# A kernel's whole order of steps and its PSUM pairs replaced by another order: RWKV-7 attention and a SwiGLU layer on one Trainium2 core

## The chip, the core and the metric

The kernel runs on one core of a Trainium2 chip as one launch. The metric is the device time of a run in microseconds (us); lower is better. Engines are named as in the profile: PE is the matrix engine (PEld its weight loads), DVE the vector engine, ACT the scalar engine, POOL the GpSimd engine, SP the engine that here only issues DMAs. A trailing "q" (SPq) is that engine's instruction queue.

## The reference

All data is fp32, but for the three weight arrays of the second part, whose 64-bit floats the kernel turns into fp32 itself.

```python
# r, k, v, w, a, b: (4, 8, 768, 40) = batch, heads, steps, head dimension
for t in range(S):
    y[:, :, t] = einsum('bhd,bhde->bhe', rt, state)
    Sa = einsum('bhde,bhe->bhd', state, at)
    state = state * wt[:, :, None, :] - einsum('bhd,bhe->bhde', Sa, bt) + einsum('bhd,bhe->bhde', vt, kt)
x = y.transpose(0, 2, 1, 3).reshape(3072, 320)
xn = x / sqrt(mean(x * x, -1) + 1e-6) * rms_g
g, val = xn @ w_gate, xn @ w_val            # (320, 1536) each
out = (g * sigmoid(g) * val) @ w_out        # (1536, 320)
```

## The kernel before, in words

The 768 steps of the recurrence are cut into 24 chunks of 32 steps. Each chunk has three stages. `front` loads the chunk's tokens (tiles `wan`, `kbn`, `wn`, `VU`), turns them with PE transposes, and builds by five levels of doubling the decayed keys and the Gram matrices of the chunk (tiles `K`, `A`, `Ab`, `KN`, `T`, `LT`); at its end LT goes through memory (`sB`) into another layout (`M`). `inverse` copies the constant tile `eye` into `Yi` on ACT and solves a 32-step triangular system in many small DVE operations on `Yi` and `tmp`; the result goes back through memory (`sY`) into LT. `main` carries the state over, solves for the chunk's updates on PE, forms the outputs `y` level by level with masks (`msi`, `msk`), takes their root mean square with a `pow` on POOL (tile `ss`), and lays the normed tokens into `xg`.

The second layer, `feed`, takes the tokens of one or two chunks at a time, in 13 groups (one chunk, eleven times two, one chunk). For each of 12 slices of d_ff it multiplies with the gate and value weights into PSUM (`ps<-xg,wf`), applies Silu on ACT (`sg`), multiplies on DVE (`hT`) and accumulates the output product in a PSUM tile of its own (`po<-wf,hT`).

The weights come as 64-bit floats. `narrow` (L964) loads the raw words of one half of a slice, and takes the exponents apart and rebuilds fp32 with five DVE operations and three ACT operations. There are 24 such halves, numbered from 0; the loads of halves 0 to 3 go through SP's queue, those of halves 4 to 23 through POOL's. Later halves reuse a later slice's tile as their raw buffer, so a load may wait until an earlier half has been narrowed. Once the weights are in, POOL issues nothing but the chunks' token loads and one `pow` per chunk.

Constants and the padding of tiles are made at the start by short POOL fills, copies and selects (`blank` L461, `pcopy` L458, `select` L484). Among them are ten 64x16 copies from `msk` into `msi` and four selects that make `eye`. Nothing fixes when they come, other than their users.

None of these stages issues an instruction when it is written down. Each operation becomes a piece in a list (class `Plan`, L205) with its engine and the pieces it needs; in all there are 5,993 pieces: 2,717 on DVE, 1,113 on ACT, 1,091 on PE (groups of 4 to 64 matmuls), 588 on POOL, 484 on SP. `Plan.issue` (L282) then issues them in the order of a constant, `ORDER` (L32): each word counts from the first piece not yet issued.

```python
for word in order.split():
    i = first + int(word)
    gone.add(i)
    while first in gone:
        first += 1
    p = self.pieces[i]
    assert not p.missing
```

The order of the words decides what stands in each engine's queue, and in what order; each engine works its queue off strictly from the front, so that a waiting instruction holds up all behind it. Semaphore waits follow from what each piece reads and writes. A second constant, `PAIRS` (L185), holds one digit, 0 to 2, for each of the 495 uses of PSUM outside `po`: which of three pairs of PSUM banks that use takes. The next use of a pair must wait until the engines have read the last one's contents. There is no other planner at run time: the two constants were found ahead of time and stand in the source as numbers.

Of the kernel before, what the change touches and what calls it, by code (L numbers as in the profile page):

```python
# [32 lines left out]
76 84 83 86 75 71 2 3 4 5 6 7 0 35 47 0 17 54 64 0 0 51 0 35 0 55 0 0 67 68 60 190 191 41 49 374 59 71 375 0  # L33
35 0 0 0 46 359 380 185 73 0 32 170 171 181 75 74 73 0 1 27 3 0 368 2 0 352 373 343 173 2 167 166 342 72 80 73 85 84 96 69
70 78 83 94 74 365 79 40 53 353 62 371 61 366 354 64 51 52 374 54 81 15 93 75 82 76 92 95 91 367 86 89 90 63 183 77 100 344 168 39
165 297 298 88 104 184 102 106 97 87 105 101 198 108 98 107 348 345 103 185 190 113 99 346 16 656 668 175 176 9 5 31 109 112 368 355 369 116 114 117
115 118 120 119 110 111 347 186 187 122 356 299 359 349 203 370 350 191 657 18 665 4 357 188 197 284 19 17 28 375 121 71 196 376 667 666 43 382 285 377
358 123 202 379 201 213 30 0 401 171 652 41 199 359 379 198 360 25 191 123 300 299 210 124 125 126 127 213 128 211 301 129 192 130 209 203 131 193 132 221
208 206 402 392 654 391 382 390 205 133 207 134 181 657 170 5 194 377 223 219 135 222 136 214 217 137 218 138 204 216 230 393 139 380 225 411 140 141 215 410
413 142 143 226 144 145 383 146 147 148 149 150 151 224 412 234 663 384 235 236 152 385 386 237 168 387 153 155 662 154 156 394 388 403 389 407 395 404 238 239  # L40
240 396 180 414 415 405 406 6 43 318 7 13 433 22 408 398 676 157 432 179 418 399 419 241 416 397 409 229 188 158 159 160 161 400 228 417 452 31 453 244
420 441 443 245 246 434 247 248 444 677 227 242 435 436 243 442 249 220 250 251 252 438 253 254 464 463 169 437 285 454 461 0 460 253 254 437 255 453 284 256
438 456 454 285 286 287 257 482 0 250 251 435 643 447 252 436 449 473 283 280 253 254 281 450 282 255 223 493 256 439 257 258 259 260 261 494 651 437 292 455
438 262 22 662 263 264 440 293 441 456 661 660 1 296 475 457 483 459 479 284 303 458 482 299 460 298 484 285 300 485 461 297 648 665 476 304 302 306 305 222
307 309 477 301 495 310 502 505 650 503 478 664 499 311 221 313 312 266 267 265 268 270 314 504 23 315 486 496 497 763 316 480 271 269 272 764 317 822 821 481
487 498 832 819 676 500 318 488 506 319 490 320 766 544 489 663 501 669 491 507 321 767 322 545 833 768 769 770 536 508 535 829 670 677 323 492 675 682 771 820
525 324 671 772 775 510 680 681 773 692 668 774 534 524 509 325 778 679 678 693 690 688 672 686 765 689 691 673 687 683 779 828 533 16 2 831 827 674 294 699
694 697 511 700 512 526 701 824 830 834 649 823 295 698 702 703 685 527 528 705 684 546 695 782 838 658 0 204 370 380 211 378 203 511 333 205 212 215 206 216
389 390 391 228 467 463 462 460 382 213 381 459 465 464 475 476 214 221 398 222 470 385 383 457 458 388 392 395 393 394 466 461 224 384 469 386 223 217 225 471
450 468 474 752 230 451 226 399 400 401 402 403 404 405 406 407 408 409 410 751 499 249 749 762 759 411 472 412 387 413 473 414 517 250 761 513 415 477 518 416  # L50
417 478 760 418 419 479 420 421 480 422 423 481 424 425 426 427 482 614 615 516 617 510 227 229 509 750 428 629 515 514 396 520 429 431 430 630 432 528 521 397
526 527 522 532 530 529 533 534 523 544 524 531 537 536 541 525 542 538 540 535 543 539 436 434 545 549 553 548 0 553 549 434 545 555 432 550 560 546 554 556
565 566 567 551 558 250 557 230 234 235 518 254 255 231 232 251 617 564 568 571 570 765 615 618 619 233 252 236 559 620 253 770 621 453 569 256 574 771 259 630
257 623 258 260 757 499 575 576 577 578 579 580 581 582 583 584 585 586 587 588 589 590 591 592 593 594 595 596 622 625 624 626 627 597 598 454 746 632 634 633
747 269 764 635 631 0 637 481 0 1 0 478 399 669 679 668 515 558 565 555 516 177 670 556 517 518 519 400 401 181 520 671 178 402 672 564 522 523 521 524
563 562 574 557 477 566 182 179 180 403 567 183 561 568 560 559 573 572 569 570 571 575 576 577 578 579 783 184 844 854 842 841 843 784 682 744 684 685 528 525
526 840 678 852 527 786 683 186 580 187 689 479 404 697 488 407 406 489 696 787 188 788 789 688 690 702 190 849 848 857 405 700 785 713 851 853 839 191 189 701
581 695 790 710 858 791 582 192 850 712 691 583 698 795 584 711 794 724 193 733 709 792 699 847 793 585 692 194 708 798 196 707 693 799 703 195 706 694 723 717
714 719 722 718 704 705 725 715 721 730 0 725 585 715 733 5 196 6 719 734 7 730 726 1 727 736 0 733 6 198 799 0 194 0 547 798 46 799 194 805
0 730 796 543 719 47 728 190 192 803 729 722 798 42 731 799 806 43 44 801 805 48 49 802 795 797 804 50 807 0 763 0 763 689 690 691 692 693 694 695  # L60
767 765 764 766 686 696 768 697 1067 769 803 687 698 770 0 943 942 694 800 766 695 799 767 41 1075 696 802 697 805 1064 698 48 47 813 806 803 1065 1063 1073 699
818 700 817 42 43 0 768 767 1030 657 757 0 4 769 770 784 657 762 5 658 774 0 779 658 762 770 780 775 46 782 791 778 659 781 660 763 776 661 53 52
47 49 54 0 43 759 657 772 784 658 769 659 779 783 788 660 782 661 787 790 662 45 785 664 663 781 50 780 789 791 684 794 665 0 687 746 754 749 639 975
752 753 755 45 0 702 41 424 52 967 42 59 0 572 4 5 710 708 15 382 1 709 384 6 10 7 711 11 383 714 0 10 15 780 11 16 0 573 571 572
570 591 796 799 798 592 780 931 913 717 712 719 713 714 721 715 716 723 718 720 0 0 0 766 781 630 767 914 907 904 631 706 709 710 0 767 905 682 768 0
619 709 710 711 712 713 714 715 716 717 718 719 720 721 722 1 364 894 768 3 769 0 0 1 408 405 341 406 0 356 357 405 358 359 235 311 360 0 414 235
3 360 415 361 236 362 237 363 364 238 365 418 366 367 0 367 428 368 419 394 369 1 430 418 370 238 371 0 0 368 427 0 0 414 418 419 417 421 415 416
423 420 426 430 367 368 543 369 427 431 428 544 545 429 724 370 371 0 431 738 306 432 728 371 538 433 732 434 0 371 434 720 372 538 0 731 434 372 373 0
734 550 537 373 2 376 374 375 377 378 0 718 554 541 2 720 3 542 537 565 727 553 4 725 311 6 547 548 715 730 551 543 312 550 726 552 576 555 563 562
716 560 561 558 723 564 559 7 557 570 544 8 379 9 545 575 380 571 574 13 546 595 378 569 556 566 577 567 568 12 578 584 572 585 582 0 581 9 576 10  # L70
582 5 568 0 568 577 572 383 217 6 579 219 384 569 581 422 578 12 423 220 580 424 654 218 652 425 520 426 653 14 509 655 8 656 585 7 586 587 588 590
589 13 9 591 592 427 593 657 594 595 0 654 591 593 655 594 5 653 10 595 596 597 598 599 600 601 602 603 604 605 606 607 608 609 610 388 658 389 611 577
659 12 578 662 673 663 664 675 668 612 669 665 613 666 667 614 670 671 13 18 14 19 615 676 682 15 20 616 617 618 16 619 620 621 674 672 989 622 677 623
678 680 681 624 679 625 626 982 992 991 979 980 505 981 683 627 628 684 514 629 0 0 0 4 613 668 614 669 615 670 671 616 617 702 706 842 703 575 704 618
619 620 717 707 716 621 709 6 12 722 710 622 624 715 711 623 705 721 719 718 7 733 729 727 744 712 720 731 843 625 728 723 725 730 9 732 713 738 726 13
8 743 14 714 742 737 739 626 734 749 724 10 629 627 745 15 735 639 736 746 748 740 755 747 763 754 756 0 0 962 678 688 741 697 629 742 617 833 661 395
398 397 749 746 748 662 396 747 0 0 657 681 943 954 814 815 658 961 724 829 830 951 828 953 659 626 734 962 671 393 817 0 951 626 817 1 943 398 3 820
# [969 lines left out]
```

## Time and profile before

| | |
|---|---|
| median of 3 runs | 1016.63 us (1014.07 to 1021.52) |
| the profiled execution | 1023.57 us |
| its span, first to last instruction | 1021.8 us |
| mean granted PE clock | 0.943 |
| PE, PEld, DVE, ACT, POOL busy | 930.1, 759.6, 771.4, 509.7, 350.0 us |
| instructions | 55,373 |

"Busy" is the time in which an engine worked on at least one instruction. Matmuls overlap, and their ends are modelled, so PE may be busy and still not at its fastest. In answers of the timeline, a row has the start, the duration, the engine, the source line, the operation, output and input tiles, and in square brackets the engine's idle time before it with what ended it. L423 is the helper that issues nearly all DVE operations, L466 the one that issues DMAs, L469 the one for matmuls and L472 the one for transposes, so it is the tiles that tell one operation from another.

### The profile page before, as it was taken

To read this page: it belongs to the slowest core of one execution; us is meant where nothing else is said; L and a number is where in the kernel's file an instruction comes from. 1 tells how busy PE (TensorE), PEld (TensorE's weight loads), DVE (VectorE), ACT (ScalarE), POOL (GpSimd) and SP (SyncE) were. 2 spreads that over 40 slices of the span, in tenths; PEclk is the share of its full clock that TensorE was granted. 3 is DMA by queue.
4 is the path that set the end of the run, shared out by engine and by line. 5 is a ranking of instruction groups with operands and counts; after the bars stand their busy time and mean duration, and the time that the engine had idled before them with its cause. 6 is when DMAs were issued, how large, how long until landed. Compare 5 with 4: busy or idle time off the path is not lost.

```text
span 1021.8 us, 55373 instructions
## 1 busy us (share of the span) xinstructions
PE 930.1 (91%) x24512; PEld 759.6 (74%) x24512; DVE 771.4 (75%) x2718; ACT 509.7 (50%) x1133; POOL 350.0 (34%) x595
## 2 busy tenths in 40 slices
PE   4366688999989999999999999999999999999998
PEld 4255577878767787788788777778787878788877
DVE  8889877787867966877769779679598697685531
ACT  6788467445445544465353454454544545435121
POOL 8988363242324314315133143143133224210000
PEclk9557767999999999999999999999999999999999
DMA  8574453323324324133232142242232323320100
GB/s 172 149 190 115 96 110 74 68 47 60 54 58 78 56 53 75 36 71 61 45 81 44 44 95 39 55 84 49 43 72 51 75 50 66 67 35 7 43 8 20
DMA packets 140175, 68.87 MB, mean 67 GB/s; under 512 B 120768, under 2 KB 127264, under 8 KB 139936
## 3 DMA queue, kind: packets, MB, share of 16 engines
q0 software_dynamic: 19680, 32.48, 15.9%
q1 hardware_dynamic: 118080, 32.54, 15.4%
q8 instruction: 192, 3.15, 1.3%
q10 hardware_dynamic: 2176, 0.33, 0.2%
q14 instruction: 47, 0.39, 0.1%
HBM read 55.05 MB, written 10.22 MB: 64 GB/s over the span
## 4 chain that ended last, share of the span: by engine, by line
PE 55%; DVE 24%; DMA 7%; issue 5%; POOL 4%; ACT 3%; SPq 2%; DVEq 0%; ACTq 0%; POOLq 0%
PE ps L469 40%; PE po L469 10%; PE ps L472 5%; DVE Yi L423 4%; DVE LT L423 3%; DVE y L423 3%; DVE tmp L423 3%; DVE K L423 3%; DMA sB<-LT 3%; SPq L466 2%; DVE As L423 2%; DMA M<-sB 2%; DVE Ab L423 1%; POOL wf L466 1%; DVE hT L423 1%
## 5 line engine op out<-in xcount | busy, mean ns | idle before, releaser
L469 PE MATMUL ps<-xg,wf 128*128 128x256 f32 (+3 forms) x1872 | 364.5, 377 | 1.5 <-ACT sg L446 0.8
L469 PEld LDWEIGHTS ps<-xg,wf 128*128 128x128 f32 (+1 forms) x1872 | 271.1, 191 | 48.6 <-issue 8.1
L469 PE MATMUL po<-wf,hT 128*128 128x320 f32 x576 | 179.0, 444 | 0.2 <-issue 0.2
L469 PEld LDWEIGHTS po<-wf,hT 128*128 128x128 f32 x576 | 103.5, 189 | 35.6 <-issue 1.4
L423 DVE TENSOR_TENSOR tmp<-Yi,M 128x24 f32<-128x24 f32 (+21 forms) x512 | 107.2, 209 | 12.1 <-DMA M<-sB 1.6
L423 DVE TENSOR_TENSOR Yi<-Yi,tmp 128x24 f32<-128x24 f32 (+21 forms) x512 | 106.8, 209 | 10.4
L423 DVE TENSOR_TENSOR hT<-ps,sg 128x256 f32<-128x256 f32 (+1 forms) x156 | 60.6, 399 | 63.7 <-PE ps L469 41.4
L446 ACT ACTIVATE sg<-ps 128x256 f32<-128x256 f32 (+1 forms) x156 | 54.5, 368 | 103.3 <-PE ps L469 102.4
L466 POOL DMA_DIRECT2D kbn<-in_k_dram x92 | 53.6, 585 | 146.9 <-PE ps L469 146.2
L466 POOL DMA_DIRECT2D kbn<-in_b_dram x92 | 53.8, 587 | 131.2 <-PE ps L469 130.1
L423 DVE TENSOR_TENSOR K<-K,T 128x256 f32<-128x256 f32 (+1 forms) x191 | 92.8, 499 | 3.7 <-PE ps L469 2.8
L469 PE MATMUL ps<-Ab,K 64*60 64x56 f32 (+2 forms) x4608 | 79.4, 224 | 17.5 <-ACT r L450 4.8
L469 PEld LDWEIGHTS ps<-Ab,K 64*60 64x60 f32 (+2 forms) x4608 | 72.6, 136 | 29.0 <-issue 9.3
L423 DVE SCALAR_TENSOR_TENSOR Yi<-M,Yi 128x31 f32<-128x31 f32 (+6 forms) x228 | 43.2, 243 | 66.7 <-DMA out_dram<-o 23.3
L450 ACT COPY KN<-ps 128x640 f32<-128x640 f32 x95 | 65.6, 692 | 46.7 <-PE ps L472 12.9
L466 POOL DMA_DIRECT2D VU<-in_v_dram x92 | 54.1, 590 | 88.0 <-PE ps L469 86.3
L423 DVE TENSOR_TENSOR As<-ps,msi 128x256 f32<-128x256 f32 (+1 forms) x168 | 70.7, 455 | 11.9 <-PE ps L469 7.0
L469 PEld LDWEIGHTS ps<-As,KN 128*40 128x40 f32 x3072 | 67.3, 128 | 15.2 <-issue 5.3
L469 PE MATMUL ps<-As,KN 128*40 128x32 f32 x3072 | 72.0, 208 | 6.1 <-DVE As L423 2.9
L466 POOL DMA_DIRECT2D wn<-in_w_dram x92 | 52.4, 571 | 69.6 <-DVE KN L423 65.4
L450 ACT COPY K<-K 128x512 f32<-128x512 f32 x95 | 60.2, 634 | 23.7 <-PE ps L469 10.9
L456 POOL TENSOR_TENSOR ss<-ss,mhalf 128x1 f32<-128x1 f32 x24 | 18.1, 755 | 147.1 <-DVE ss L423 146.9
(137 smaller groups left out, 1526.4 us busy)
## 6 DMA issues: line engine op xcount, KB each, us to landing
M<-sB SPq DMA_DIRECT2D x96, 128.0 KB, 2.9
wan<-in_r_dram SPq DMA_DIRECT2D x24, 160.0 KB, 4.2
kbn<-in_b_dram POOLq DMA_DIRECT2D x92, 40.0 KB, 2.5
VU<-in_v_dram POOLq DMA_DIRECT2D x92, 40.0 KB, 2.7
wan<-in_w_dram POOLq DMA_DIRECT2D x46, 80.0 KB, 3.0
wan<-in_a_dram POOLq DMA_DIRECT2D x46, 80.0 KB, 2.8
kbn<-in_k_dram POOLq DMA_DIRECT2D x92, 40.0 KB, 2.7
wn<-in_w_dram POOLq DMA_DIRECT2D x92, 40.0 KB, 2.9
```

Of the source, the lines that this page charges most:

```text
L423: plan.add("DVE", time + more + each * size(o), 0.087, lambda at: [fn(at(o), *m(at))], [o], aps(*args))
L446: scalar(o, [a], lambda at: nc.scalar.activation(at(o), at(a), f, **kw), aps(acc), 0.1 if f in (AF.Square, AF.Relu) else 0.0)
L450: scalar(o, [a], lambda at: nc.scalar.copy(at(o), at(a)), extra=more)
L456: plan.add("POOL", 0.5, 0.06, lambda at: nc.gpsimd.tensor_tensor(o, a, b, op), [o], [a, b])
L466: plan.add(by, 0.6 if by == "POOL" else 0.45, 0.0, lambda at: queue.dma_start(out=o, in_=i), [o], [i], load=load, since=since)
L469: return o, lhsT, rhs, lambda at: nc.tensor.matmul(at(o), lhsT, rhs, start=start, stop=stop, skip_group_check=True), 4
L472: return o, i, ident, lambda at: nc.tensor.transpose(at(o), i, ident), 2
```

## The change

`ORDER` and `PAIRS` hold other numbers. All 150 lines of the order and all 5 of the pairs change: of the order's 5,993 words 279 are the same at the same position. Nothing else in the file differs; the list of pieces, what each does and what each needs is the same. The order was searched anew as a whole, the early part included, with twelve draws of noise at a time and with a model in which the PE clock follows the work. The diff, cut to the first and last lines of each constant:

```diff
 ORDER = """
-76 84 83 86 75 71 2 3 4 5 6 7 0 35 47 0 17 54 64 0 0 51 0 35 0 55 0 0 67 68 60 190 191 41 49 374 59 71 375 0
...
+388 86 84 2 61 75 3 0 80 81 70 3 4 45 5 6 24 191 200 75 71 84 73 57 7 8 82 26 193 0 78 370 0 5 56 40 0 0 0 375
...
+31 20 0 0 8 0 10 5 18 31 0 13 19 0 13 3 15 9 0 0 0 0 5 0 2 4 0 0 0 2 0 0 0
 PAIRS = """
-212020210212120201011000000002122102121202002110201212101120120100121021022021021012211022112120021122201112110120220200
...
-112220222120210
+100101122202001210212110021002002202122111102010210202010120220121021021020101021021021212221210210012121221002020020200
...
+202001002210021
```

What the new numbers do to each engine's queue is told where the prediction needs it.

More of the change, by code (lines that the diff above doesn't have):

```diff
@@ L32 @@
 ORDER = """
[150 rows of a table removed]
[150 rows of a table added]
 """
 PAIRS = """
-212020210212120201011000000002122102121202002110201212101120120100121021022021021012211022112120021122201112110120220200
-211101012202202011120000200020220222022111222002110010201111111221020101112100110011110120101220200212221202210202000120
-200001010122101111022221020102022012211212111120001012110101122002220000222011120101011110101020010100212121202001201010
-202022202022012001121220211222122020022201202021101121220111201111101001012220112210102111212102000010100200202021210201
-112220222120210
+100101122202001210212110021002002202122111102010210202010120220121021021020101021021021212221210210012121221002020020200
+110121011220020200010212121110110111211000222221002101201022202221012021020202020221012120012121211101102020020122101221
+210110101211202220201120121011020011120020221111010120201212210022020011110000212020022221202120002021222121212112121211
+212121010020120200010100011010100102212121020212101001020100102220110001021220110120202011012120012121210220212022001201
+202001002210021
 """
```

297 rows, old and new, of the table ORDER are left out of this document.

## The prediction

> **What bounds the kernel now.** I read the page first, then the busy time by stretches, then the chain that ended last, then the waits of single instructions in the timeline.
>
> ```profile
> span 1021.8 us, 55373 instructions
> PE 930.1 (91%) x24512; PEld 759.6 (74%) x24512; DVE 771.4 (75%) x2718; ACT 509.7 (50%) x1133; POOL 350.0 (34%) x595
> PE   4366688999989999999999999999999999999998
> PEclk9557767999999999999999999999999999999999
> PE 55%; DVE 24%; DMA 7%; issue 5%; POOL 4%; ACT 3%; SPq 2%; DVEq 0%; ACTq 0%; POOLq 0%
> ```
>
> The kernel has two regimes. The fortieths are 25.5 us each: for the first seven PE is half busy and its granted clock lies between 0.5 and 0.8 (the first slice apart), after that PE is busy throughout at full clock. Shares over the whole span hide this, so here are the stretches (columns: stretch, its length, busy time of each engine, clock, DMA).
>
> ```profile
> 0.00:51.00 51.00, 20.46 (x678) 18.56 (x680) 45.49 (x139) 34.40 (x61) 45.58 (x85) 0.77 0.72 160
> 51.00:102.00 51.00, 32.08 (x1303) 28.73 (x1301) 45.40 (x131) 41.75 (x81) 43.01 (x69) 0.63 0.63 153
> 102.00:153.00 51.00, 37.08 (x1415) 33.42 (x1411) 41.89 (x139) 28.73 (x61) 24.47 (x42) 0.66 0.47 103
> 153.00:204.00 51.00, 47.05 (x1483) 41.41 (x1487) 37.74 (x126) 31.14 (x74) 15.99 (x28) 0.90 0.34 71
> ...
> 408.00:510.00 102.00, 99.18 (x2502) 79.47 (x2501) 79.78 (x311) 47.98 (x110) 28.71 (x49) 1.00 0.27 52
> ...
> 970.00:1022.00 52.00, 47.24 (x646) 38.40 (x644) 12.65 (x36) 11.61 (x33) 0.55 (x1) 0.99 0.06 14
> ```
>
> Up to 102 us DVE (45.5 and 45.4 of 51) and POOL (45.6 and 43.0 of 51) are the full engines. From 204 us on PE is: 99.2 of 102 in the stretch shown. So a reordering can save in two places: DVE's idle time before 204 us, which is 5.51 + 5.60 + 9.11 + 13.26 = 33.5 us by these rows, and the few per cent that PE idles later. The chain shows that the early bound is not DVE alone:
>
> ```profile
> 28.86 0.22 POOL msi L459
> 29.09 3.54 issue
> 32.62 0.73 POOL wf L466
> ...
> 50.55 4.14 DMA wf<-in_moe_w_gate_dram
> ```
>
> From 28.9 to 54.7 us everything that ended last was POOL's queue: fills of tiles, small copies and the issue of weight loads one behind the other, and at its end a load that lands just as DVE needs it. The timeline says why POOL was late (square brackets: idle time before it and what ended it):
>
> ```profile
> 7.30 0.65 POOL L466 DMA_DIRECT2D wan<-in_w_dram  x1 [1.38 <-PE ps L472]
> 9.91 0.33 POOL L459 COPY msi<-msk 64x16 f32<-64x16 f32 x1
> 27.53 0.74 POOL L466 DMA_DIRECT2D wf<-in_moe_w_gate_dram  x1 [2.46 <-DVE A L423]
> 28.51 0.68 DVE L423 TENSOR_TENSOR K<-K,T 128x512 f32<-128x512 f32 x1
> 28.86 3.81 POOL L459 COPY msi<-msk 64x16 f32<-64x16 f32 x1
> 32.62 0.73 POOL L466 DMA_DIRECT2D wf<-in_moe_w_gate_dram  x1
> ```
>
> The same 64x16 copy took 0.33 us at 9.91 and 3.81 us at 28.86, where DVE ran one operation on two tiles behind another. With the two waits for a free buffer, 1.38 and 2.46 us, POOL lost 7.3 us ahead of the load at 50.55.
>
> **The change, part by part.** No instruction is added or taken away: both programs have the same 13,464 matmuls, 2,717 planned DVE steps, 1,113 of ACT, 588 of POOL and 484 of SP. What moves, counted in the two orders with the durations of this execution:
>
> *Balance.* By the first step of feed 0, DVE has done 171.0 us of its work in the old order and 171.8 in the new, and PE 62.6 and 62.6 (at its median late pace). By the last step of feed 1 it is 285.5 and 280.0. PE's sequence has 537 runs of one stage before and 545 now. So the plan is the same and this is a local shuffle: DVE steps move by about 1 us, PE steps by 2 to 6. A gain or loss of tens of microseconds has no source here.
>
> *DVE, early.* I counted the DVE steps that stand less than 2 us of DVE work behind the step of another engine that they need, within the first 172 us of DVE work: 85 before, 58 now. Each is a place where a small lateness stops DVE and all behind it. The largest waits of before show what was done:
>
> ```profile
> 39.39 0.29 DVE L423 TENSOR_TENSOR Ab<-Ab,T 128x128 f32<-128x128 f32 x1 [2.34 <-PE ps L469]
> 69.22 0.76 DVE L423 TENSOR_TENSOR As<-ps,msi 128x256 f32<-128x256 f32 x2 [1.31 <-PE ps L469]
> 88.19 0.74 DVE L423 COPY_PREDICATED LT<-near,ps 128x384 f32<-128x384 uint32 x1 [1.94 <-ACT VU L450]
> 105.39 0.42 DVE L423 TENSOR_TENSOR y<-y,ps 128x256 f32<-128x256 f32 x1 [0.95 <-ACT y L450]
> 134.04 0.19 DVE L423 TENSOR_TENSOR tmp<-Yi,M 128x30 f32<-128x30 f32 x1 [1.58 <-DMA M<-sB]
> 162.68 0.75 DVE L423 COPY_PREDICATED LT<-near,ps 128x384 f32<-128x384 uint32 x1 [1.13 <-PE ps L469]
> 200.38 0.29 DVE L423 TENSOR_TENSOR hT<-ps,sg 128x128 f32<-128x128 f32 x1 [3.04 <-ACT sg L446]
> ```
>
> Ahead of the first four the new order puts 1.26, 2.55, 2.15 and 4.15 us more DVE work, enough for 1.26 + 1.31 + 1.94 + 0.95 = 5.5 us of them; ahead of the last three it puts nothing, or takes work away. Done for all 25 early waits over 0.25 us (25.6 us together), the work put ahead covers 12.9 us. That is the best case, because the work put ahead was taken from another place, where a wait can open. From the other side the number of tight places gives 33.5 x (1 - 58/85) = 10.6 us. The worst case without a new mechanism is 0: waits that only change place. I take half of 10.6, **-5.3 us**, because DVE's total is unchanged and the balance at feed 0 is the same in both orders.
>
> *POOL, early.* Two things go for it. The 3.81 us copy moves from 24.4 to 8.0 us of POOL work, ahead of the dense DVE stretch; at 0.33 us it saves 3.5. The loads that waited 1.38 and 2.46 us now stand 7.1 and 8.6 us of POOL work later, so those waits should end. Against it: loads of weights go back in POOL's queue. The gate load of half 4 (the first whose loads POOL issues) has 31.8 us of POOL work ahead instead of 23.2, half 7's last 44.2 instead of 39.8, half 8's (the one at 50.55) 48.0 instead of 46.3, halves 16 to 18 some 5 us more. At half 8 the sum is +1.7 - 1.38 - 2.46 - 3.5 = -5.6 us at best, +1.7 at worst. Since DVE waits for this load, the gain is part of the 5.3 above and not added to it: **0**.
>
> The Trainium skill has the reason for the 3.81 us in "GPSIMD Engine Reference", section 8 (Key points): GpSimd shares its SBUF interfaces with VectorE and contends with DVE instructions that have two SBUF inputs. The trace agrees (0.33 against 3.81 us). The rule also speaks against the change, as the first rival shows.
>
> *PE, late.* Here cover got thinner. PE steps less than 1 us of DVE work behind what they need, after that same 172 us: 70 before, 81 now; PSUM pairs handed on with no PE work between the last read of the old contents and the first write of the new: 132 of 492 before, 144 now. What such waits cost PE after 204 us (us in total, times, longest):
>
> ```profile
> PE ps L469 <- issue: 6.4, 8, 2.3
> PE ps L469 <- DVE hT L423: 3.1, 3, 2.6
> PE ps L469 <- DVE LT L423: 2.9, 8, 0.5
> PE ps L472 <- DVE hT L423: 1.2, 2, 1.0
> PE ps L469 <- DMA LT<-sY: 1.1, 1, 1.1
> PE ps L469 <- DVE As L423: 0.8, 2, 0.4
> ```
>
> Together 15.5 us. Grown by 11/70 that is +2.4 us; against that ACT's tight places fall from 304 to 289, and the lower bound is a like gain, -1.5. I take half of the upper bound, **+1.2 us**. What is queued behind such a wait is all of PE.
>
> *Clock.* PE was busy 32.1 us at clock 0.63 and 37.1 at 0.66 between 51 and 153 us. If closer packing raised 0.66 to 0.76 there, 37.1 us would shrink by some 4.9. But PE idles in these stretches (18.9 and 13.9 us) and PE's early sequence is nearly the same, so I take 0 and keep 5 on either side inside the cases below.
>
> *Sum.* The profiled execution took 1023.57 us, 6.94 above the median of the three runs, so differences are applied to both: 1023.57 - 5.3 + 1.2 = 1019.5 for that execution, 1016.63 - 4.1 = **1012.5 us** for the median.
>
> **The rivals.**
>
> *POOL starves in another place (slower, 1028 us).* In the new order two of the msi copies and three of the four selects that build `eye` stand between 23.5 and 29.8 us of POOL work. That is where DVE runs its two-tile operations back to back, and ahead of the loads of halves 4 and 6. All five read SBUF. If four of them take 3.5 us more each, and one such stall is gone, POOL is 10.5 us later; the copy of `eye` into Yi, which opens inverse 0, and then every weight load are late by that much, and DVE stops in order behind them.
>
> ```profile
> 30.75 0.41 ACT L450 COPY Yi<-eye 128x256 f32<-128x256 f32 x1
> ```
>
> The groups of both kinds of POOL instruction (count | busy us, mean ns of one | idle before):
>
> ```profile
> L485 POOL TENSOR_SCALAR_AFFINE_SELECT eye<-eye 32x256 f32<-32x256 f32 x4 | 2.4, 612 | 0.2
> L459 POOL COPY msi<-msk 64x16 f32<-64x16 f32 x10 | 6.6, 670 | 0.3
> ```
>
> 1016.63 + 10.5 + 1.2 = 1028.3. Against it: the four selects took 612 ns on average though DVE was busy 45.49 of the first 51 us, and nine of the ten copies took (6.6 - 3.81)/9 = 0.31 us. It decides from the fourth long stall on; with one or two the forecast stands.
>
> *All the cover counts (faster, 1005 us).* If the 12.9 us of covered waits come through whole and PE's late waits grow by 1.2, the time is 1016.63 - 11.7 = 1004.9. For it: the first thing that PE needs to fill up is DVE's early work. Against it: it asks that no new wait opens.
>
> *Nothing comes of it (1017.8 us).* The early waits change place, PE is full from 204 us on whatever came before, and only the +1.2 stays. For it: equal balance at feed 0.
>
> **How the numbers follow.** Forecast of a small gain 0.38, nothing 0.20, both within 1% (10.2 us, about what a measurement of this kernel can tell from no change). Full cover 0.25, which is faster by over 1%. POOL's starving and what else costs over 1%, 0.17. So faster 0.25, same 0.58, slower 0.17. The range begins with full cover and a late gain of 1.5 instead of the loss (1016.63 - 12.9 - 1.5 = 1002.2) and ends at 1025, short of the slow rival's price; about 1 in 10 lies outside on either side.
>
> **What would show it.** Right: DVE's idle time before 204 us falls from 33.5 to about 28; the 3.81 us copy is back near 0.33; the half 8 gate load is issued before 50.55; PE's late waits grow by 1 to 2 us; the first long full-clock stretch begins at nearly the same place, some microseconds earlier. Wrong: a POOL copy or select of over 3 us between 24 and 32 us, DVE waiting for POOL or for DMA of wf in the first 100 us, or PE's idle time after 204 us up by more than 5 us. Then the sum's early or late term has the wrong sign.

## The result, and the profile after

The new order is slower by a little: 1025.18 us against 1016.11 us (medians of 18 runs each), a ratio of 1.0079 with a 95% interval of 1.0052 to 1.0105. That is 8.0 us on the 1016.63 us of before; the two medians lie 9.1 us apart. The forecast was 4.1 us in the other direction. Ratios and shares, here and below, leave out single executions over 1.5% above the fastest of their kernel; medians and ranges of times keep them.

| | before | after |
|---|---|---|
| median of 18 runs (lowest to highest) | 1016.11 us (1012.96 to 1024.36) | 1025.18 us (1019.86 to 1031.31) |
| the profiled execution | 1023.57 us | 1025.81 us |
| its span | 1021.8 us | 1024.0 us |

The profiled execution of before lies 7.5 us above its own median and that of after only 0.6 above, so that the two profiles differ by 2.2 us where the kernels differ by 8.0. A loss of a few microseconds is not to be read from these two spans, only where it is local and large.

The page of after, the same rows as those shown of before (busy time, PE's busy tenths and granted clock in fortieths, shares of the chain that ended last):

```profile
PE 932.1 (91%) x24512; PEld 760.4 (74%) x24512; DVE 770.7 (75%) x2718; ACT 507.5 (50%) x1133; POOL 348.3 (34%) x595
PE   4456688999999999999999999999999999999998
PEclk9556757999999999999999999999999999999999
PE 52%; DVE 23%; DMA 7%; issue 7%; POOL 4%; SPq 3%; ACT 3%; DVEq 0%; POOLq 0%; ACTq 0%
```

Nothing shows on this scale: busy times agree within 2.3 us. The difference begins in the stretches of after (length; busy time of PE, PEld, DVE, ACT, POOL; clock; DMA):

```profile
0.00:51.00 51.00, 21.69 (x681) 19.77 (x683) 42.24 (x133) 31.98 (x57) 46.25 (x86) 0.77 0.68 148
51.00:102.00 51.00, 31.07 (x1226) 27.94 (x1226) 47.28 (x127) 41.58 (x80) 40.15 (x66) 0.63 0.63 157
102.00:153.00 51.00, 36.37 (x1340) 33.08 (x1340) 42.52 (x142) 30.85 (x63) 22.08 (x37) 0.64 0.44 99
153.00:204.00 51.00, 45.67 (x1455) 40.02 (x1451) 39.36 (x127) 29.88 (x68) 20.00 (x34) 0.83 0.34 70
```

In the first 51 us DVE was busy for 42.24 us where it had been 45.49, and it caught up later (47.28 against 45.40). Its idle time before 204 us is 8.76 + 3.72 + 8.48 + 11.64 = 32.6 us; it was 33.5. So nearly all of the 5.3 us that DVE was to gain is absent, and it lost 3.25 us in the first stretch. Nor is this idle time a measure of the loss: by 204 us DVE had even done 0.9 us more work than before (171.4 against 170.5), while the results of feed 0, shown below, came 5.6 us later.

The timeline of after says where. POOL first, with one instruction that took as long as ten of its kind:

```profile
9.15 0.19 POOL L459 COPY msi<-msk 64x16 f32<-64x16 f32 x1
...
28.11 0.65 POOL L466 DMA_DIRECT2D wan<-in_w_dram  x1 [2.19 <-PE ps L472]
28.81 6.42 POOL L485 TENSOR_SCALAR_AFFINE_SELECT eye<-eye 32x256 f32<-32x256 f32 x2
35.27 0.95 POOL L462 MEMSET rE<- 32x1024 f32 x1
```

The copy into `msi` that had taken 3.81 us is indeed at 0.19. But two selects of `eye` took 6.42 us together; taken singly, the first ran 5.94 us and the second 0.44. What stood behind them shows in the queues of ACT and DVE, first after, then before:

```profile
36.25 1.01 ACT L450 COPY rE<-ps 104x1024 f32<-104x1024 f32 x1 [4.12 <-POOL rE L462]
37.16 0.41 ACT L450 COPY Yi<-eye 128x256 f32<-128x256 f32 x1
34.02 0.43 DVE L423 TENSOR_TENSOR K<-K,T 128x256 f32<-128x256 f32 x1
37.60 0.19 DVE L423 TENSOR_TENSOR tmp<-Yi,M 128x30 f32<-128x30 f32 x1 [3.15 <-ACT Yi L450]
```

```profile
35.60 1.01 ACT L450 COPY rE<-ps 104x1024 f32<-104x1024 f32 x1 [3.83 <-POOL rE L462]
32.52 0.21 DVE L423 TENSOR_TENSOR tmp<-Yi,M 128x30 f32<-128x30 f32 x1
```

Before, ACT copied `eye` into `Yi` at 30.75, ahead of the copy into `rE`. In the new order the copy into `rE` stands ahead of it, and that one needs POOL's fill of `rE`, which stands behind the selects. So `Yi` was ready at 37.57 and DVE stood still for 3.15 us with the first operation of inverse 0, which begins at 37.60 instead of 32.52. The chain of after runs through the same four rows (start, length, what; of the first select this view counts 3.07 us, and puts the rest down to issue):

```profile
28.81 3.07 POOL eye L485
...
35.27 0.95 POOL rE L462
36.25 0.05 ACT rE L450
...
37.16 0.41 ACT Yi L450
```

How long this stays can be followed by the stores of the feeds' results, whose issues on SP's queue end each feed (feeds 0, 1 and 2; first after, then before):

```profile
214.73 1.72 SPq L466 DMA_DIRECT2D out_dram<-o  x4
290.33 1.77 SPq L466 DMA_DIRECT2D out_dram<-o  x4
371.49 3.11 SPq L466 DMA_DIRECT2D out_dram<-o  x4
```

```profile
209.18 2.02 SPq L466 DMA_DIRECT2D out_dram<-o  x4
285.44 2.11 SPq L466 DMA_DIRECT2D out_dram<-o  x4
365.67 1.87 SPq L466 DMA_DIRECT2D out_dram<-o  x4
```

The new order is 5.6 us late at feed 0, 4.9 at feed 1 and 5.8 at feed 2. At feed 3 the old order issues its four stores singly, from 435.27 to 444.34, and the new one in two pairs, at 435.51 and 436.97, so that from there on single stores no longer compare the two. Nor does one execution stand for its kernel: another trace with the old order up to 470 us (e10, below) has feed 0 at 205.46 and feed 2 at 356.94. So the parts were run by themselves.

PE's waits after 204 us in after (us in total, times, longest):

```profile
PE ps L469 <- issue: 5.2, 8, 1.2
PE ps L469 <- ACT sg L446: 1.8, 3, 0.9
PE ps L472 <- issue: 1.5, 3, 0.7
PE ps L469 <- DVE As L423: 1.1, 2, 0.6
PE ps L472 <- DVE hT L423: 1.1, 3, 0.7
PE ps L469 <- DVE A L423: 1.0, 2, 0.8
```

They sum to 11.7 us where the six largest of before had 15.5.

### The profile page after: what moved, and what is told of

Read it like the earlier page. It is cut to its first block, busy times and chain, and to the rows that moved or that the text cites. A ratio compares the mean times of both kernels' runs of the same rounds, so it can differ in the third digit from the quotient of the medians.

```text
span 1024.0 us, 55383 instructions
## 1 busy us (share of the span) xinstructions
PE 932.1 (91%) x24512; PEld 760.4 (74%) x24512; DVE 770.7 (75%) x2718; ACT 507.5 (50%) x1133; POOL 348.3 (34%) x595
## 3 DMA queue, kind: packets, MB, share of 16 engines
q8 instruction: 192, 3.15, 1.3%
## 4 chain that ended last, share of the span: by engine, by line
PE 52%; DVE 23%; DMA 7%; issue 7%; POOL 4%; SPq 3%; ACT 3%; DVEq 0%; POOLq 0%; ACTq 0%
PE ps L469 38%; PE po L469 10%; PE ps L472 5%; DVE y L423 4%; DVE Yi L423 4%; SPq L466 3%; DVE As L423 3%; DVE tmp L423 3%; DVE LT L423 2%; DMA sB<-LT 2%; DMA M<-sB 2%; DVE K L423 2%; DMA sY<-Yi 1%; DVE hT L423 1%; POOL kbn L466 1%
## 5 line engine op out<-in xcount | busy, mean ns | idle before, releaser
L469 PE MATMUL ps<-Ab,K 64*60 64x56 f32 (+2 forms) x4608 | 82.1, 227 | 19.9 <-ACT r L450 5.8
L423 DVE SCALAR_TENSOR_TENSOR Yi<-M,Yi 128x31 f32<-128x31 f32 (+5 forms) x228 | 43.1, 242 | 48.5 <-DMA M<-sB 32.6
L469 PEld LDWEIGHTS ps<-As,KN 128*40 128x40 f32 x3072 | 66.8, 128 | 15.5 <-issue 6.3
L456 POOL TENSOR_TENSOR ss<-ss,mhalf 128x1 f32<-128x1 f32 x24 | 15.6, 652 | 165.1 <-DVE ss L423 154.3
```

The costliest lines, as they stand in the source:

```text
L423: plan.add("DVE", time + more + each * size(o), 0.087, lambda at: [fn(at(o), *m(at))], [o], aps(*args))
L456: plan.add("POOL", 0.5, 0.06, lambda at: nc.gpsimd.tensor_tensor(o, a, b, op), [o], [a, b])
L469: return o, lhsT, rhs, lambda at: nc.tensor.matmul(at(o), lhsT, rhs, start=start, stop=stop, skip_group_check=True), 4
```

## The experiments

**Where the loss sits.** The theory: the loss is made before 180 us, by POOL's starved selects and what is queued behind them, and carried to the end. The rival: it is made later, by new waits between PE, ACT and DVE. The two orders hold the same set of pieces in their first 1,123 words (up to some 180 us) and again in their first 2,903 (some 470 us), so their parts can be exchanged at these two seams. The digits of `PAIRS` go with their part (in some of these kernels with the pairs' numbers exchanged, so that a pair fits across the seam). Written with the two orders as lists:

```diff
-ORDER = old[0:1123] + old[1123:2903] + old[2903:]
+ORDER = new[0:1123] + old[1123:2903] + old[2903:]   # e1_first_new
+ORDER = old[0:1123] + new[1123:2903] + new[2903:]   # e2_rest_new
```

> The first 1,123 pieces (to about 180 us, the same set of pieces in both orders) in the new order, the other 4,870 in the old one. Theory (two eye selects on POOL starve at 28.8 us, inverse 0 starts 6.4 us late, and the lag stays to the end): 5 to 6.5 us slower than before, 1021 to 1023. Rival (the loss is made after 180 us by thinner cover of PE and the other PSUM pairs): as before, within 1.5 us.

> The first 1,123 pieces in the old order, the rest with its PSUM pairs in the new one. Theory: what is left of the 9 us, 2.5 to 4 us slower than before, 1018.5 to 1020. Rival (late loss): 8 to 9 us slower, 1024 to 1025. If the late part of the new order is as good as the old one: within 1.5 us of before.

> The kernel before, unchanged, as a control and for a second profile. All theories: ratio 1.00 within 0.3%. In the first profile of it the granted clock fell to half for 3.4 us at 297, 400 and 727 us; if those belong to that one execution, this profile has fewer, and a span near 1014.

e4_old_again is the kernel before without any edit, as a measure of what this comparison can tell. All against 1016.96 us of before on that chip:

| | median | ratio | interval |
|---|---|---|---|
| new up to 1,123, old behind | 1025.33 us | 1.0074 | 1.0040 to 1.0108 |
| old up to 1,123, new behind | 1026.47 us | 1.0080 | 1.0048 to 1.0112 |
| before again | 1017.98 us | 1.0024 | 0.9989 to 1.0059 |

Either part alone costs as much as the whole change. So the early part is guilty, and the rest too, which the theory had put at 2.5 to 4 us, and the two losses do not add up: 0.74% and 0.80% apart, 0.79% together.

The second profile of before, taken from e4_old_again, fell on its slowest execution (1027.17 us). Its span is 1025.4 us and not the 1014 that were expected of it, and the clock falls to 0.50 again near 297 and 731 us, though not near 400.

**The parts by themselves.** To get rid of what the rest does, the program is cut off at the seams; everything behind the cut, and with it most of the output, is left out.

```diff
-        for word in order.split():
+        for word in order.split()[:1123]:    # e5_old_1123, e6_new_1123
+        for word in order.split()[:2903]:    # e7_old_2903, e8_new_2903
```

> Only the first 1,123 pieces of the old order (all else, the whole output included, is left out): how long the early part takes by itself. By its trace the old order is through these at about 180 us; with launch and drain some 185 to 200 us. It is the base for the next kernel.

> The same 1,123 pieces in the new order, all else left out. Theory (the early part loses by POOL's starved selects, in every execution): 5 to 7 us over the old order's. Rival (the early lag is one of the profiled execution; the loss comes later): within 2 us of the old order's.

> Only the first 2,903 pieces of the old order (the same set as in the new one; four groups of the output's thirteen are written, the rest left out). By the profiles some 480 us. It is the base for the next kernel.

> The same 2,903 pieces in the new order. By the two profiles the early lag of 5.5 us is caught up by 440 us: then within 1.5 us of the old order's. If it is not caught up in the executions without that lucky stretch, 5 to 9 us over the old order's; then the middle of the old order is what is faster in the timed runs than in its profile.

| | median (lowest to highest) | share of before, interval |
|---|---|---|
| old, 1,123 words | 182.87 us (181.95 to 185.21) | 0.1793 (0.1785 to 0.1801) |
| new, 1,123 words | 189.26 us (187.10 to 189.48) | 0.1854 (0.1844 to 0.1865) |
| old, 2,903 words | 474.19 us (469.17 to 478.98) | 0.4637 (0.4611 to 0.4663) |
| new, 2,903 words | 478.68 us (474.54 to 482.46) | 0.4698 (0.4671 to 0.4725) |

The early part loses 6.4 us, and of that 4.5 us are left at 470 us. This is no matter of which execution was profiled: the runs of the two short kernels don't overlap. The starved select is in the new one's trace again, as is its price on DVE:

```profile
28.76 6.46 POOL L485 TENSOR_SCALAR_AFFINE_SELECT eye<-eye 32x256 f32<-32x256 f32 x2
37.58 0.19 DVE L423 TENSOR_TENSOR tmp<-Yi,M 128x30 f32<-128x30 f32 x1 [3.15 <-ACT Yi L450]
```

In the old one the copy into `msi` that had taken 3.81 us stands at nearly the same time with the same operations on DVE, and takes 0.72:

```profile
28.82 0.72 POOL L459 COPY msi<-msk 64x16 f32<-64x16 f32 x1
```

So how long such an instruction starves differs between two executions of one order. Over all traces that have the old order of POOL up to there, this copy took 3.80 to 3.89 us in six and 0.71 or 0.72 in four. The select of the new order took 5.94 to 6.09 us in all four traces that have it.

**The middle and the end alone.**

```diff
-ORDER = old[0:1123] + old[1123:2903] + old[2903:]
+ORDER = old[0:1123] + new[1123:2903] + old[2903:]   # e9_mid_new
+ORDER = old[0:1123] + old[1123:2903] + new[2903:]   # e10_end_new
```

> Pieces 1,124 to 2,903 (about 180 to 470 us) in the new order with its PSUM pairs, the rest in the old one. If the new order is worse late in one place, this or the next kernel shows nearly all of the 9 us of the kernel with the whole rest new, 1024 to 1026, and the other is as before within 2 us. If the loss is spread over the late part, each shows about half, 1020 to 1022.

> Pieces from 2,904 on (after 470 us) in the new order with its PSUM pairs, those before in the old one. Loss in one place: 1024 to 1026 here or in the kernel above, and the other one within 2 us of before. Loss spread: 1020 to 1022 in both.

Against 1011.17 us of before on that chip: the middle alone 1018.14 us, ratio 1.0066 (1.0035 to 1.0097); the end alone 1017.19 us, ratio 1.0042 (1.0004 to 1.0080). Each of the three parts costs by itself, 0.74%, 0.66% and 0.42% (the last is little more than the 0.24% that the unchanged kernel showed), and together they cost 0.79%. A lag that is made early is thus not simply carried to the end, and what a part costs depends on what it follows.

**Is it the starved select?** The four selects go straight behind the fill of `eye`, ahead of DVE's dense stretch; all else stays as in the new order. Once whole, once cut at 1,123 words (the rest left out).

```diff
 # POOL's queue, by pieces
 fill eye
+select eye, select eye, select eye, select eye
 ...
-select eye   # one at 16.66 us, one at 24.43, two at 28.81
```

> The new order with one thing moved: the four selects that make eye stand right behind the fill of eye in POOL's queue (at about 16 us), not two of them at 28.8 us. Theory: each takes under 0.8 us there, the copy of eye into Yi comes at about 31 us as before the change, and the kernel is 4 to 6 us faster than the new order, 1019 to 1021. Rival (weight loads stand later in POOL's queue, which alone makes narrowing late): under 1.5 us faster than the new order, 1024 to 1025.

> The first 1,123 pieces of the new order with the four selects of eye right behind its fill; all else, the output included, left out. Theory (the starved selects are the early loss): 3.5 to 5.5 us under the new order's 189.3, so 184 to 186. Rival (the weight loads that stand later in POOL's queue are): 188 to 189.5.

The whole kernel took 1026.72 us, ratio 1.0086 (1.0051 to 1.0121): nothing regained, where 4 to 6 us were expected. Yet in its trace nothing stalls (the last of the `msi` copies before the fill of `rE`, the first inverse operation, and the stores of feeds 0 and 2):

```profile
25.78 0.26 POOL L459 COPY msi<-msk 64x16 f32<-64x16 f32 x1
33.61 0.18 DVE L423 TENSOR_TENSOR tmp<-Yi,M 128x30 f32<-128x30 f32 x1
210.53 2.08 SPq L466 DMA_DIRECT2D out_dram<-o  x4
372.28 3.08 SPq L466 DMA_DIRECT2D out_dram<-o  x4
```

It is 4.2 us ahead of after at feed 0 and 0.8 us behind it at feed 2, in an execution of 1027.07 us. The early stall was avoided here, and by these two executions what came of it was gone again before 375 us. That agrees with e2, where the old first part in front of the new rest did not help either.

The cut one took 184.32 us (182.61 to 189.35), share 0.1823 (0.1813 to 0.1834): by the shares, 0.0031 of the 0.0061 that the new order had lost, half; by the times 4.9 of 6.4 us, on another chip. Its profiled execution stands apart: it took 189.35 us, as long as the new order, and the five others 182.61 to 184.97. Its trace shows how the whole loss can come back (POOL, then DVE):

```profile
16.18 2.03 POOL L485 TENSOR_SCALAR_AFFINE_SELECT eye<-eye 32x256 f32<-32x256 f32 x4
26.20 7.79 POOL L459 COPY msi<-msk 64x16 f32<-64x16 f32 x1
35.30 0.95 POOL L462 MEMSET rE<- 32x1024 f32 x1
33.52 0.41 DVE L423 TENSOR_TENSOR K<-K,T 128x256 f32<-128x256 f32 x1
37.63 0.19 DVE L423 TENSOR_TENSOR tmp<-Yi,M 128x30 f32<-128x30 f32 x1 [3.70 <-ACT Yi L450]
```

The selects now take 2.03 us, all four. The next instruction that reads SBUF, the copy that took 0.26 us in the whole kernel, starved in their place, and the fill of `rE` was as late as ever. The last DVE operation of the dense stretch ends at 33.93, and the starved copy at 33.99; in after these are 34.45 and 34.75, in before 32.60 and 32.67. In these executions the starved instruction came through when DVE's stretch of long operations was over, so its price was what was left of that stretch. In the new order the stretch ends only when DVE has run out of work that does not need POOL. What is missing of the loss in the five other executions this trace cannot tell.

**Is starving enough?** The other way round: the old order, cut at 1,123 words (the rest left out), with the copy into `msi` moved to 10 us and two selects of `eye` put in its place at 28.9 us. The copy into `Yi` stays ahead of the one into `rE`.

```diff
 # POOL's queue of the old order, by pieces
+copy msi     # near 10 us
 ...
-select eye, select eye
 ...
-copy msi     # 28.86 us
+select eye, select eye
```

> The first 1,123 pieces of the old order with three POOL pieces exchanged: two selects of eye stand where the msi copy of 3.8 us stood (28.9 us), and that copy goes ahead to 10 us; all else left out. Theory: the two selects take 5 to 7 us there, Yi<-eye comes at 34 to 36 us, and it ends 2 to 5 us over the old order's 182.9, at 185 to 188. Rival (place of the selects does not matter, POOL has slack): 182 to 184.

It took 183.11 us (180.61 to 184.25), share 0.1796 (0.1783 to 0.1809): no loss against 0.1793, where 2 to 5 us were expected. In the one traced execution, of 183.50 us, the selects starve:

```profile
28.38 4.51 POOL L485 TENSOR_SCALAR_AFFINE_SELECT eye<-eye 32x256 f32<-32x256 f32 x2
32.93 0.41 ACT L450 COPY Yi<-eye 128x256 f32<-128x256 f32 x1 [2.38 <-POOL eye L485]
33.37 0.19 DVE L423 TENSOR_TENSOR tmp<-Yi,M 128x30 f32<-128x30 f32 x1 [1.26 <-ACT Yi L450]
```

`Yi` comes 0.4 us behind the selects, and DVE waits 1.26 us instead of 3.15. Two late selects alone cost little: the traced execution of e5, where nothing starved for long, took 183.53 us. Three of the other executions here took 180.61 to 182.72 us, and whether their selects starved is not known, so that a price of up to some 2 us is not ruled out. The larger price must come from what is queued between them and `Yi`: in the new order the fill of `rE` and the copy into `rE`, and a longer dense stretch (5.94 us left of it instead of 4.03).

**All of it taken out.** The new first part with all selects and the three late `msi` copies straight behind the fill of `eye`, and the fill of `rE` straight behind that of `r`; once with the old rest, once cut at 1,123 words (the rest left out).

```diff
 # POOL's queue of the new order, by pieces
 fill eye
+select eye x4, copy msi x3
 ...
 fill r
+fill rE
 ...
-copy msi x3, select eye x4, fill rE   # from their later places
```

> The first 1,123 pieces in the new order with POOL's readers out of the dense stretch (the four selects of eye and the three msi copies still open stand behind the fill of eye at 16 us, the fill of rE behind that of r at 24 us), the rest in the old order. Refined theory (any POOL piece that reads SBUF between 26 and 33 us starves, and in the new order the fill of rE, the rE copy and then Yi<-eye on ACT are queued behind it): the early lag is gone, 1016 to 1019, within 3 us of before. Rival (the rest of the new early order is slower as well, or a new first part costs the old rest its pace): 1022 to 1025.

> The same first 1,123 pieces alone, all else left out. Refined theory: within 1.5 us of the old order's 182.9, and no POOL piece over 2 us before 35 us. Rival (POOL's later weight loads): 185 or more.

The cut kernel took 184.78 us (183.48 to 185.86), share 0.1826 (0.1814 to 0.1838), 1.9 us over e5 where at most 1.5 were expected. The starving is gone from its trace, and `Yi` is ready at 31.98:

```profile
16.18 2.20 POOL L485 TENSOR_SCALAR_AFFINE_SELECT eye<-eye 32x256 f32<-32x256 f32 x4
30.66 1.01 ACT L450 COPY rE<-ps 104x1024 f32<-104x1024 f32 x1
31.57 0.41 ACT L450 COPY Yi<-eye 128x256 f32<-128x256 f32 x1
```

By the shares it has back (0.1854 - 0.1826)/(0.1854 - 0.1793) = 46% of the early loss, by the absolute times 70%; the chips differ. The traced execution has all of it back: 183.48 us, where the traced one of e5 took 183.53 and that of e6 189.48. Of e14's other three, one took 183.71 us and two took 185.85 and 185.86. With the old rest it took 1015.23 us, before 1012.02, ratio 1.0035 (1.0003 to 1.0067), where the unmended first part had 1.0074 (1.0040 to 1.0108). That too is half, but the two intervals overlap. What the slower two executions of e14 lose has no cause found.

**Does the old order gain from the same medicine?** Old order, the 3.81 us copy moved to 10 us, nothing else.

```diff
 # POOL's queue of the old order, by pieces
+copy msi     # near 10 us
 ...
-copy msi     # 28.86 us
```

> The old order with one piece moved: the msi copy that took 3.8 us at 28.9 us goes ahead to 10 us in POOL's queue. Theory (the starved POOL piece costs the old order too): 1 to 3.5 us faster than before. Rival (the weight load behind it waited for nothing that is late, or the next reader starves in its place): within 1 us of before.

1012.10 us against 1012.02, ratio 0.9988 (0.9959 to 1.0018): nothing, where 1 to 3.5 us were expected. In the old order the stall costs nothing that the time shows.

**The middle: order or PSUM pairs?** Old first part and new middle, cut at 2,903 words (the end left out); then the same with 55 of the middle's 153 PSUM uses given to the pair that has been free for longest; and the old order with the same cut on the same chip.

```diff
-ORDER = old[0:1123] + old[1123:2903]                            # e18_old_2903_again
+ORDER = old[0:1123] + new[1123:2903]                            # e15_oldnew_2903
+ORDER = old[0:1123] + new[1123:2903], 55 uses on another pair   # e17_oldnew_other_pairs_2903
```

> The first 1,123 pieces in the old order, 1,124 to 2,903 in the new one, all else left out. Theory (the new order has its own slower pace between 180 and 470 us, which an early lag hides behind): 3.5 to 6.5 us over the old order's 474.2, as late as the wholly new one. Rival (times add up, so the new middle gains what the new start loses): 0 to 3 us under the old order's.

> The first 1,123 pieces in the old order, 1,124 to 2,903 in the new one, as in e15, but each PSUM use of the middle takes the free pair that was left longest ago: 55 of the middle's 153 uses follow another one than the new pairs say. All else left out. If the new pairs make the middle slow: 2 to 5 us under e15 (ratio 0.4703), so 0.465 to 0.468. If the order does: as e15, 0.469 to 0.472, or slower.

> The first 2,903 pieces of the old order once more, all else left out, on the same chip as the kernel above. All theories: the ratio of e7, 0.464 within 0.003; its distance to e17 is what order and pairs of the new middle cost.

The new middle with its own pairs took 475.98 us, share 0.4703 (0.4676 to 0.4730); with other pairs 476.08 us, share 0.4657 (0.4633 to 0.4682); the old order 475.40 us, share 0.4656 (0.4631 to 0.4681). The last two, on one chip, are the same. The one with its own pairs ran on a chip where the kernel before was faster (1012.02 against 1018.61 us), and its absolute time is that of the second. By the shares the pairs would be the cause, by the times they make no difference. The traces side with the times: e15 and e17 (476.79 and 477.95 us) store feed 2 at 370.22 and 371.32, and e18 at 363.15, though it is hardly faster in the end. This stays open.

## Why the prediction was wrong, point by point

**Early DVE, -5.3 us: wrong sign.** This is the step that failed. Counting places where DVE stands close behind its supplier said that 85 places had become 58. But a place is not a price: one place that got worse, `Yi` behind `rE` behind the selects, cost a wait of 3.15 us and put inverse 0 back by 5.1 us, and the early part lost 6.4 us in all. Nor was the gain hidden under the stall: with the stall taken out, the new early order is level with the old one in the traced executions (183.48 against 183.53 us) and 1.9 us behind it by the medians (e14 against e5). DVE's idle time before 204 us, forecast at 28, is 32.6. DVE's largest waits before 204 us in after are (us in total, times, longest):

```profile
DVE LT L423 <- PE ps L469: 5.0, 7, 1.6
DVE tmp L423 <- DMA M<-sB: 3.7, 2, 2.3
DVE tmp L423 <- ACT Yi L450: 3.2, 1, 3.2
```

The first two had been 4.0 and 1.6 us in the same view of before, and the third was not there; the wait of 2.34 us ahead of `Ab` is gone. That is the prediction's worst case, waits that only change place, and a new mechanism on top.

**Early POOL, 0: wrong.** Moving POOL's pieces alone gave back 4.5 of the 6.4 us by the medians and 6.0 us in the traced executions (e14 against e6, on different chips). The two things that spoke for POOL came true: the copy fell to 0.19 us, and the two loads that had waited for a free buffer started without a wait, at 10.10 and 36.75. But another `wan` load now waits 2.19 us, at 28.11. The gate load of half 8, to start before 50.55 if the gain came, is issued at 53.15, past the bound of +1.7 us, and DVE waits a little more for it than the 0.25 us of before:

```profile
53.15 0.78 POOL L466 DMA_DIRECT2D wf<-in_moe_w_gate_dram  x1
57.76 0.41 DVE L423 TENSOR_SCALAR o<-wf 128x480 int32<-128x480 int32 x1 [0.71 <-DMA wf<-in_moe_w_gate_dram]
```

But by then `Yi` had already cost its 3.15 us. What mattered first was which instruction of another engine stands behind which POOL piece, and the sum had looked only at weight loads.

**The rival "POOL starves in another place": right in its place and mechanism, wrong in price and in the point from which it decides.** It named the selects of `eye`, the stretch and the copy into `Yi`. It took 3.5 us for each of four instructions and let the rival decide from the fourth long stall on. In after a single instruction stalled, for 5.94 us, and that sufficed. The stalls do not add up one by one: the first to stall takes what is left of DVE's dense stretch, and those behind it run when the stretch is over (0.44 us for the second select). And the price at the end was not the stall but the queue behind it: with a stall and `Yi` next in line it cost nothing to some 2 us (e12); with a longer stall, and `rE` in between as well, it cost about half of 6.4 us or more (e14 against e6). The rival's 1028.3 us is 3.6 us above what 1.0079 makes of 1016.63 us; part of the closeness is chance, since its term of 10.5 us stood for 6.4 early.

The Trainium skill, "GPSIMD Engine Reference", section 8 (Key points), says that GpSimd contends with VectorE for its SBUF interfaces where DVE reads two inputs. The traces agree: what starved were the reading instructions (5.94 us for a select of 0.44, 7.79 us for a copy that took 0.26 in e3), while in after the fill of `LT` at 25.39 took 0.52 us and the issue of the load at 28.11 took 0.65 us. In the same stretches stood single DVE operations that read one tile (0.41 us, as at 29.86 and 32.09 in after), and the select did not come through there.

**Late PE, +1.2 us: too small.** The new middle alone cost 0.66% and the new end alone 0.42%, some 6.7 and 4.3 us of 1016.63. Behind the new first part they cost together some 0.5 us (0.79% less 0.74%) to 1.6 us (the 8.0 of the whole less the 6.4 of the first part by itself), both within the noise. The sign that was to show it, PE's waits grown by 1 to 2 us, pointed the wrong way: 15.5 us fell to 11.7 in the six largest rows. The base itself was not sound: late waits differ between executions of one order by more than the forecast. One wait of DVE in before, and the same in e10, which has the same order up to 470 us:

```profile
289.44 2.48 DVE L423 SCALAR_TENSOR_TENSOR Yi<-M,Yi 128x27 f32<-128x27 f32 x12 [8.07 <-DMA out_dram<-o]
```

```profile
281.94 2.48 DVE L423 SCALAR_TENSOR_TENSOR Yi<-M,Yi 128x27 f32<-128x27 f32 x12 [4.73 <-DMA M<-sB]
```

DVE waited 8.07 us in one and 4.73 in the other for LT's way through memory into `M` (the first row names the store queued right behind M's loads, which took 4.3 to 4.7 us to land). The multiplication into `hT` stands behind it, and PE behind that: the 2.6 us in the row of before's waits. In the six traces with this order up to there (in e16 but for one POOL copy), the wait is 6.85 to 8.19 us in four and 4.71 and 4.73 in two. The six largest rows of PE's waits sum to 15.5 us in before and to 16.7 in the second trace of the same kernel (e4), but to 11.3 in e16. So the fall to 11.7 shows no gain, and scaling the six rows by a count of tight places asked more of one execution than it can tell.

**Clock, 0:** the first stretches have 0.77, 0.63 and 0.64 against 0.77, 0.63 and 0.66, as taken. From 153 to 204 us it is 0.83 against 0.90, with PE busy for 45.67 us instead of 47.05: there the lag shows, PE fills up later.

**What stays open:** what is left of the early loss by the medians (in e14 and e13), the mechanism of the middle's and the end's losses, and why three losses of 0.74, 0.66 and 0.42% make 0.79% together. The stall-free e3 is as slow as after: the stall accounts for half or more of the early 6.4 us, but taking it away leaves the 8.0 us of the whole as they are. One thing that would fit, a slack that any one delay uses up and that further delays then share, was not tested.

## What to carry to other kernels

When an order is rearranged, do not count close places; follow for each late piece of a small engine who stands behind it in the other engines' queues, and price the longest such chain (here select, fill, copy, copy, DVE). Keep small POOL instructions that read SBUF out of stretches where DVE runs two-tile operations back to back, or take the rest of that stretch as the price of the first of them. And before a sum of a few microseconds is made against one profiled execution, see where that execution stands among the runs; parts of a new order have to be run alone and together, since their losses need not add, and a gain made early (4.2 us at feed 0 in e3) can be gone 160 us later.

## What the runs showed of the hardware that was not expected

A POOL instruction of 0.2 to 0.4 us took 3.81, 5.94 and 7.79 us beside DVE operations on two tiles, and in three traces came to its end within 0.3 us of the end of DVE's dense stretch. In four of ten traces with the same order of POOL the copy of 3.81 us was done in 0.71 or 0.72 us, so that the stall is likely, not certain. In these four it ended within 0.03 us of the end of a two-tile DVE operation (29.51 against 29.49 in e4) that a one-tile operation followed; in the other six it did not come through there.

The spread of one kernel is wider than most edits here: before ran from 1005.91 to 1027.17 us over all chips, and its median differed between chips from 1011.17 to 1018.82 us. Times of cut kernels did not follow the full kernel's from chip to chip: e15 took 475.98 us beside 1012.02, e17 476.08 beside 1018.61.
